# Chunk 0's scores over 128 rows with zero products between them, and raw weights that are loaded, measured and split at other steps

## The chip, the core and the metric

The kernel runs on one core of a Trainium2 chip. The metric is device time in microseconds. Three runs of the kernel before took 908.86, 908.33 and 905.04 us, so the median is 908.33 us. One further execution was profiled. It took 909.34 us, and its span from the first to the last instruction is 907.6 us.

The core has five engines that work beside each other: TensorE (PE, matrix products and transposes; its weight loads are the row PEld), VectorE (DVE), ScalarE (ACT), GpSimd (POOL) and SyncE (SP, which issues the transfers here). Each goes through its own list of instructions in a fixed order.

## The reference

Attention with a forget gate and causal mask, for 4 batches, 8 heads, 576 positions and head size 64, and behind it a mixture of 4 experts over the 2304 rows:

```
scores = scale * np.matmul(q, k.transpose(0, 1, 3, 2))
decay = cum[:, :, :, None] - cum[:, :, None, :]      # cum: running sum of log f
scores = np.where(causal, -1000000000.0, scores + decay)
attn = softmax(scores)                               # written out in the reference
x = (attn @ v), heads side by side                   # 2304 x 512
out += p[:, e:e+1] * (np.maximum(x @ w1[e], 0.0) @ w2[e])   # for e in 4 experts, w1 512x1024
```

All inputs and the output are float32.

## The kernel before

**Chunks and heads.** Rows are cut into nine chunks of 256. Chunks 0 to 3 are the first 256 positions of the four batches, chunks 4 to 8 the rest. The attention of a chunk is done by heads, two heads to a `Job`. Chunk 0 belongs to the first eight heads, h0 to h7 below (`FIRST` = 8).

**Startup.** `startup()` does chunk 0 in an order written out by hand. A head goes through: scores on PE (`qk_pe`, L631), their minimum on DVE (`qk_min`, L647), the exponential on ACT (`qk_exp`, L662), three transposes on PE (`tr_pe`, L768), a copy of these out of PSUM (`tr_copy`, L776 on ACT for even heads, L778 on DVE for odd ones), and the product with v (`av_pe`, L784). Two heads later a spread of the row sums follows (`spread`, L712). In turn s PE's list has the scores of head s+1, the transposes of head s and the v product of head s-1. For chunk 0 the decay is the 65th row of the operands: the tiles `first` hold 64 rows of q and k and one row of decays, and the scores are float32 products over these 65 rows. Ahead of all that `awake()` issues 18 products of zeros on PE.

**Experts, first sweep.** The weights of an expert come in four groups a half, a group in four units of 128x1024 (512 KB each). A `Step` is one half group on one chunk: first product (`l1`, L985 or L997), relu, second product (`l2`, L1040). The first `WIDE` = 4 groups (units 0 to 15) are used on chunk 0 as float32, straight from the loaded unit. For every later group a raw unit is loaded (`w_load`), the largest absolute value of it is taken on DVE (`w_top`, L310, or in halves through spare tiles), the four maxima give a scale (`w_scale`), and then `w_split` writes two float16 parts with ACT (L954) and DVE (L955). The steps count n = 0, 1, 2 ...; steps 0 to 7 are the wide ones, step 8 begins group 4.

**What sets the order.** Behind startup a scheduler places instructions, held back where the code says `issue_after`. `PACE` says which head's attention has begun by which step. Raw units live in two rings of four buffers, "wr" and "wk"; before, units 20 to 23 stand in two of the first, with two units in tiles of the accumulator. The list `loaded` with its step decides when a maximum is taken. `normalize()` (L458 to L461) turns the router's probabilities into shares on DVE; nothing before the end of the first step uses them. All transfers go through SP's one list, and each waits there for its buffer.

Of the kernel before, what the change touches and what calls it, by code (L numbers as in the profile page):

```python
# [19 lines left out]
CH = 256  # L20
# [63 lines left out]
def fused(ctx: ExitStack, tc: tile.TileContext, qk, v, f, probs, w, out):  # L84
# [57 lines left out]
    def awake():  # L142

        t = zero.bitcast(F16)
        ps = ps_a.tile([128, 512], F32, tag="a", name="awake")
        for _ in range(18):
            nc.tensor.matmul(out=ps, lhsT=t[:, :128], rhs=t, start=True, stop=True)

    def decays():
        nc.vector.memset(zero, 0.0)  # L150
        nc.sync.dma_start(out=fr, in_=f)
        first_tiles()
        first_raw(0)
# [13 lines left out]
        nc.gpsimd.memset(ones_r, 1.0)  # L167
        for n in range(1, NPR):
            nc.gpsimd.memset(jobs[n].whole[64:65, :, :CH], 8.0)
        for t in q2:  # L170
            nc.gpsimd.memset(t[64:66, :].bitcast(F32), 8.0)
        nc.vector.memset(ones, 1.0)
        nc.vector.tensor_scalar(
            out=fr, in0=fr, scalar1=1e-4, scalar2=1.0, op0=ALU.max, op1=ALU.min
        )
        for a, z in ((0, CH), (CH, S)):
            nc.scalar.activation(out=fr[:, a:z], in_=fr[:, a:z], func=AF.Ln)
            nc.vector.tensor_tensor_scan(
                out=ncum[:, a:z],
                data0=ones[:, a:z],  # L180
                data1=fr[:, a:z],
                initial=ncum[:, a - 1 : a] if a else 0.0,
                op0=ALU.mult,
                op1=ALU.subtract,
            )
            if a == 0:
                first_row(0)
# [130 lines left out]
    def w_peek(i):  # L318

        g, k = divmod(i, 4)  # L320
        t = xf_p.tile([128, 1024], F32, tag=f"xf{2 + i % 2}", name=f"wp{i}")
        nc.sync.dma_start(out=t, in_=w[i])
        at_step(step + 2, lambda: w_top(g, k, t))
        if k == 3:
            at_step(step + 2, lambda: scale(g))

    def w_half(i, k):

        g, n = divmod(i, 4)
        t = x_p.tile([128, 512], F32, tag="x", name=f"wp{i}_{k}")  # L330
        nc.sync.dma_start(out=t, in_=w[i, :, 512 * k : 512 * k + 512])

        def top():
            nc.vector.tensor_reduce(
                out=wmax[:, slot(g), k, n : n + 1],
                in_=t,
                op=ALU.max,
                axis=AX.X,
                apply_absolute_value=True,
            )  # L340

        at_step(step + 2, top)
        if (n, k) == (3, 1):
            at_step(step + 3, lambda: scale(g))

    def scale(g):
        a_, b_, c_ = w_scale(g)
# [117 lines left out]
    def first_tiles():  # L465

        slots = [
            x_.tile([128, 1024], F32, tag=t, name=f"first{n}")
            for n, (x_, t) in enumerate([(xf_p, f"xf{k}") for k in range(3)] + [(acc_p, "acc")] * 2)
        ]  # L470
        firsts["v"] = slots[3]
        vt = firsts[0] = slots[3].rearrange("p (r t h d) -> p r t h d", r=NPR, t=2, h=2)
        for j in jobs[:NPR]:
            r = slots[(4, 0, 1, 2)[j.pr]]
            j.whole = r.rearrange("p (h n) -> p h n", h=2)
            j.raw = {hh: j.whole[:, hh] for hh in range(2)}
            j.vr = vt[:, j.pr]
        nc.gpsimd.memset(jobs[0].whole[64:65, :, :CH], 8.0)

    def first_raw(n):  # L480
        j = jobs[n]
# [28 lines left out]
    class Job:  # L510
# [99 lines left out]
        def qk_pe(self, hh, its):  # L610

            at = 512
            for t in its:
# [3 lines left out]
                for n, (a, z) in enumerate(cuts):  # L617
# [282 lines left out]
        return st + qs + us  # L900


    wh, wl, wraw, loaded = {}, {}, {}, {}
    NS = 4 * len(GROUPS)

    def unit(n):
# [8 lines left out]

    def w_load(n):
        if n < 4 * WIDE and n not in wraw:
            if n % 4 < 2:
                wraw[n] = w_p.tile([128, 1024], F32, tag="w", name=f"w{n}")
            else:  # L920
                wraw[n] = wr_p.tile([128, 1024], F32, tag=("wr", "wk")[n % 2], name=f"wr{n}", bufs=4)
# [1 line left out]
                gate.append(nc.sync.dma_start(out=wraw[n], in_=w[unit(n)]))  # L923
        elif n in RAWS and n not in wraw:
            i = RAWS.index(n)
            if i in (6, 7):
                wraw[n] = acc_p.tile([128, 1024], F32, tag="acc", name=f"wr{n}")
            else:
# [4 lines left out]
            loaded[n] = step  # L933

    def w_pair(n):
        t = w_p.tile([128, 2, 1024], F16, tag="w", name=f"w{n}")
# [6 lines left out]
    def w_split(n):  # L943
# [22 lines left out]
        if i < len(RAWS):  # L966
            w_load(RAWS[i])

    acc = {}
# [500 lines left out]
    ]  # L1470
    starts = [next(n for n, t in enumerate(steps) if t.s == s) for s in range(len(GROUPS))]

    EARLY = (starts[-1] + 3, starts[-1] + 5)
    done_at = {}
    for n, (j, _) in enumerate(heads):
# [39 lines left out]
    def pace(n):  # L1515
# [8 lines left out]
            m += 1  # L1524
        upto(m)

    def startup():

        J = lambda h: heads[h] if 0 <= h < FIRST else (None, None)
# [6 lines left out]
            heads[0][0].qk_min(0, t)  # L1536
        for s in range(FIRST + 2):
            (m, mm), (j, hh), (i, ii), (k, kk) = J(s + 1), J(s), J(s - 1), J(s - 2)
            if s == 1:
                bound[2]()  # L1540
            if s == 2:
                bound[3]()
            if m:
# [2 lines left out]
                m.qk_pe(mm, m.its)  # L1546
                for t in m.its:
                    m.qk_min(mm, t)
            if j:
                for t in j.its:  # L1550
                    j.qk_exp(hh, t)
# [3 lines left out]
                j.tr_pe(hh)  # L1555
            if i:
                i.tr_copy(ii)
                i.av_pe(ii)
                if ii:
                    i.recip()  # L1560
# [1 line left out]
                k.fin()  # L1562
            if s == 0:
                bound[0]()
                bound[1]()
            for n in {0: (0, 1, 2), 1: (3,), 3: (4, 5)}.get(s, ()):
                w_load(n)
            if s == 0:
# [20 lines left out]
    for n in range(len(steps) + 1):  # L1589
# [4 lines left out]
        if 0 <= n - V_PEEK < NV:  # L1594
            v_peek(n - V_PEEK)
        with tc.issue_after(gate[-1].ins):
            if n < 4:
                w_peek(4 * WIDE + n)
            if n == 0:
                w_load(RAWS[6])  # L1600
                w_load(RAWS[7])
        for i, m in W_PEEK:
            if 0 <= n - m < 8:
                w_half(i + (n - m) // 2, (n - m) % 2)
        if cur is not None:
# [5 lines left out]
                weigh(cur.g, cur.c)  # L1611
            if n == 5:
                narrow_0()
            due = [m for m in loaded if WIDE < m // 4 < SWEEP_1 and loaded[m] < n][:2]
            off = starts[s] + (len(GROUPS[s][1]) > 1)
            turn = next((k for k in range(WIDE, SWEEP_1 - 1) if n == starts[k] - 1), None)
            if turn:
                due += [m for m in loaded if m // 4 == turn + 1 and m not in due]
            for m in due:
                del loaded[m]  # L1620
                behind(lambda: w_top(GROUPS[m // 4][0], m % 4, wraw[m]))
            chain = None
            if turn:
                chain = w_scale(turn + 1)
                behind(chain[0])
            for q in range(4):
                cur.l1(q)
# [26 lines left out]
        if cur is not None:  # L1654
            if chain:
                chain[2]()
            s = cur.s
            for k in range(2):
                if n == off + k and WIDE <= s + 1 < len(GROUPS):
                    with tc.issue_after(cur.last.ins):  # L1660
                        for i in range(2):
                            w_split(4 * s + 4 + 2 * k + i)
            if n < 7:
                for i in range(2):
                    w_load(2 * n + AHEAD_W + i)
            if n == starts[WIDE - 1]:
                w_load(RAWS[4])
                w_load(RAWS[5])
# [95 lines left out]
```

## Time and profile before

| | |
|---|---|
| three runs | 905.04, 908.33, 908.86 us, median 908.33 |
| profiled execution | 909.34 us, span 907.6 us |
| PE busy | 874.5 us, 96% of the span |
| DVE busy | 681.1 us, 75% |
| ACT, POOL busy | 511.2 us and 363.1 us |
| TensorE's granted clock, mean | 0.986 of full speed |

The page's second part cuts the span into 40 slices and gives the busy share of each engine and the granted clock in tenths. [...] The clock's column shows 1.0 until its first event, whatever it was before. The records of a matmul overlap with the next one's, so the time of one is read from start to start.

### The profile page before, as it was taken

Reading aid. Unit: us, or ns where it says so; the run is one execution under the profiler, and the core shown is the slowest. Engines: PE = TensorE matmul, PEld = TensorE weight load, DVE = VectorE, ACT = ScalarE, POOL = GpSimd, SP = SyncE. Lnnn points to the kernel's source line nnn. Section 1 sums busy time; section 2 is a strip of 40 time slices with the busy share of each in tenths; the row PEclk is TensorE's granted clock in tenths of the full one; section 3 lists DMA queues with packets and bytes.
Section 4 is the critical chain, followed back from the end, with each engine's and each line's share of the span. In section 5 each row is a group of like instructions: output and inputs, shape, how many; then the busy total and the mean of one; then the engine's idle time right before and its main releaser. Section 6 shows DMA issues by size and latency. Waiting matters only on the chain.

```text
span 907.6 us, 16252 instructions
## 1 busy us (share of the span) xinstructions
PE 874.5 (96%) x5681; PEld 562.2 (62%) x5681; DVE 681.1 (75%) x1483; ACT 511.2 (56%) x1063; POOL 363.1 (40%) x416
## 2 busy tenths in 40 slices
PE   6999979999999999999999999999989999999998
PEld 3666656666666766666676666644456654666547
DVE  4466779888888899877878985846788647886486
ACT  3354653566766885666668664456655445654350
POOL 2233421434232243232232220756788437884160
PEclk7699999999999999999999999999999999999999
DMA  7996796887999989896998964171223432240003
GB/s 225 405 223 178 218 278 166 242 277 204 285 236 223 230 285 317 200 216 151 256 281 230 288 117 101 47 256 69 94 71 116 139 117 70 70 139 25 24 0 94
DMA packets 166306, 162.50 MB, mean 179 GB/s; under 512 B 104824, under 2 KB 129456, under 8 KB 166224
## 3 DMA queue, kind: packets, MB, share of 16 engines
q1 hardware_dynamic: 166224, 161.46, 64.4%
q8 instruction: 45, 0.74, 0.3%
q14 instruction: 37, 0.30, 0.1%
HBM read 115.65 MB, written 21.64 MB: 151 GB/s over the span
## 4 chain that ended last, share of the span: by engine, by line
PE 25%; POOL 12%; DVE 8%; ACT 7%; issue 4%; DMA 2%; POOLq 0%; ACTq 0%; SPq 0%; DVEq 0%
PE y L1275 6%; PE m L1275 6%; PE l L997 5%; PE l L1040 5%; POOL s L1335 4%; POOL wt L1172 4%; POOL wu L1172 2%; PE s L631 1%; PE o L810 1%; ACT wt L1199 1%; DMA pt<-z 1%; DVE w L955 1%; DVE acc L1069 1%; DVE rl L1161 1%; ACT r L1321 1%
## 5 line engine op out<-in xcount | busy, mean ns | idle before, releaser
L997 PE MATMUL l<-y,w 128*128 128x256 f16 x1728 | 212.8, 273 | 2.5 <-DVE gl L1014 2.3
L997 PEld LDWEIGHTS <-w 128*128 128x128 f16 x1728 | 163.1, 98 | 44.7 <-issue 10.7
L1040 PE MATMUL l<-w,gh 128*128 128x512 f16 (+1 forms) x600 | 184.6, 392 | 1.1 <-DVE acc L1069 1.1
L576 POOL CAST q<-raw 64x320 fp32r<-64x320 f32 (+1 forms) x56 | 26.4, 472 | 227.2 <-issue 126.1
L662 ACT ACTIVATE p<-p,nm 128x576 f32<-128x576 f32 (+3 forms) x112 | 74.4, 665 | 73.9 <-DVE nm L647 63.8
L1040 PE MATMUL l<-w,gl 128*128 128x512 f16 x284 | 106.6, 379 | 1.3 <-DVE gl L1014 1.3
L1069 DVE SCALAR_TENSOR_TENSOR acc<-y,scg,acc 128x256 f32<-128x256 f32 (+1 forms) x164 | 81.2, 516 | 14.9 <-PE y L1275 14.7
L749 DVE SCALAR_TENSOR_TENSOR z<-p,rs,z 128x384 f16<-128x384 f32 (+3 forms) x128 | 80.1, 649 | 13.7 <-ACT z L748 11.3
L583 POOL TENSOR_TENSOR kl<-raw,hi 64x576 fp32r<-64x576 f32 (+1 forms) x56 | 65.2, 1164 | 60.1 <-ACT hi L574 56.1
L1275 PE MATMUL m<-rh,bs 128*128 128x512 f16 x256 | 86.4, 379 | 0.2 <-POOL bs L1204 0.2
L1040 PEld LDWEIGHTS <-gh 128*128 128x128 f16 x568 | 51.3, 98 | 49.2 <-issue 7.4
L647 DVE CUSTOM_DVE_ANT_0 p<-s,mask 128x384 f32<-128x384 f32 (+3 forms) x112 | 58.5, 531 | 25.0 <-PE s L631 24.4
L748 ACT ACTIVATE z<-p,rs 128x384 f16<-128x384 f32 (+3 forms) x128 | 69.7, 591 | 6.3 <-ACT p L662 2.3
L631 PE MATMUL s<-hi 128*128 128x288 f32 (+4 forms) x176 | 69.9, 409 | 1.8 <-DVE y L839 1.3
L1204 POOL TENSOR_TENSOR bs<-wt,bs 128x512 f16<-128x512 f32 x32 | 38.0, 1190 | 73.4 <-ACT bs L1203 73.0
L1275 PE MATMUL m<-rh,bw 128*128 128x512 f16 x191 | 64.5, 379 | 1.0 <-ACT r L1321 1.0
L1275 PEld LDWEIGHTS <-bs 128*128 128x128 f16 x384 | 37.5, 98 | 38.8 <-POOL bs L1204 0.7
L1009 ACT ACTIVATE gh<-l 128x512 f16<-128x512 f32 (+1 forms) x80 | 47.0, 587 | 24.3 <-PE l L997 18.3
L1014 DVE SCALAR_TENSOR_TENSOR gl<-l,gh 128x512 f16<-128x512 f32 x72 | 49.4, 686 | 14.7 <-ACT gh L1009 13.8
L1310 DVE SCALAR_TENSOR_TENSOR h<-s,h 128x512 f16<-128x512 f32 x40 | 46.3, 1164 | 17.8 <-ACT h L1309 17.5
L574 ACT ACTIVATE hi<-raw 128x896 fp32r<-128x896 f32 (+1 forms) x56 | 45.1, 810 | 23.7 <-issue 11.8
L1275 PEld LDWEIGHTS <-h 128*128 128x128 f16 x480 | 46.9, 98 | 14.8 <-issue 2.6
(386 smaller groups left out, 1750.9 us busy)
## 6 DMA issues: line engine op xcount, KB each, us to landing
wr<-in_w SPq DMA_DIRECT2D x66, 512.0 KB
wd<-w SPq DMA_DIRECT2D x32, 512.0 KB
w<-wd SPq DMA_DIRECT2D x32, 512.0 KB
raw<-in_qk SPq DMA_DIRECT2D x32, 448.0 KB
wp<-in_w SPq DMA_DIRECT2D x32, 256.0 KB
bv<-wd SPq DMA_DIRECT2D x32, 256.0 KB
bw<-wd SPq DMA_DIRECT2D x32, 256.0 KB
raw<-in_qk SPq DMA_DIRECT2D x24, 256.0 KB
```

Source lines behind the costliest of these rows:

```text
L583: nc.gpsimd.tensor_tensor(out=kl[:64, :wk], in0=r[:64, ko : ko + wk], in1=hi[:64, ko : ko + wk].bitcast(F32), op=ALU.subtract,)
L631: nc.tensor.matmul(out=ps[:, at : at + z - a], lhsT=lhsT, rhs=rhs, start=(m == 0), stop=(m == len(parts) - 1),)
L647: nc.vector.tensor_tensor_reduce(out=pt[:, a:z], in0=ps, in1=mask[:, m0 + a : m0 + z], scale=-0.125, scalar=BIG if n == 0 else nm[:, col : ...
L662: nc.scalar.activation(out=pt[:, :w_], in_=pt[:, :w_], func=AF.Exp, scale=-1.0, bias=self.nmax[hh][:, c : c + 1], accum_out=self.ssum[:, h ...
L748: nc.scalar.activation(out=o[:, 0], in_=x, func=AF.Copy, scale=sc)
L749: nc.vector.scalar_tensor_tensor(out=o[:, 1], in0=x, scalar=sc, in1=o[:, 0], op0=ALU.mult, op1=ALU.subtract)
L997: nc.tensor.matmul(out=self.l1p[:, fi, :], lhsT=lhsT, rhs=rhs[:, k, :], start=(k == 0 and m == 0), stop=(k == 3 and m == 2),)
L1014: self.last = nc.vector.scalar_tensor_tensor(out=self.gl, in0=self.l1p, scalar=0.0, in1=self.gh, op0=ALU.max, op1=ALU.subtract,)
L1040: matmul(out=l2[tt], lhsT=lhsT, rhs=rhs, start=(opens and fi == 0 and m == 0), stop=(closes and fi == 1 and m == len(parts) - 1),)
L1069: nc.vector.scalar_tensor_tensor(out=acc[c][:, tt, d0:d1], in0=ps, scalar=sc, in1=acc[c][:, tt, d0:d1], op0=ALU.mult, op1=ALU.add,)
L1172: nc.gpsimd.tensor_tensor(out=t[:, k - 1, :], in0=w_of(a), in1=w_of(z), op=op)
L1275: line.append(nc.tensor.matmul(**args))
```

## The change

- `awake()` issues 16 products of zeros and not 18.
- The tiles of chunk 0 are filled with zeros from row 64 on (four DVE memsets of 64x1024, `first_ends`), the 8.0 of row 64 is written behind that, and the scores of chunk 0 go over all 128 rows.
- `fill(ps, n)` issues n float16 products of 128x128 zeros (a corner of the mask that holds zeros) into columns 384 on of a head's transpose tile: four ahead of the transposes of each of the eight heads, four ahead of each v product; 64 in all.
- In startup the exponent chain of the first bound moves: its transposes (`bound[1]`) stand behind the scores of h2, its second product behind the v product of h0 (`bound[2]`).
- `normalize()` is held back until startup's last instruction.
- Raw units alternate over both rings. Units 16 and 17 are loaded at step 0, 18 and 19 at step 2, 20 and 21 at step 4, 22 and 23 at step 6 (`LOADS`). Splits of group 4 go to steps 3 and 4, of group 5 to steps 8 and 9 (`SPLITS`). Maxima stand at steps of a table (`TOPS`, `SCALES`), of four units through spare tiles. Units 14 and 15 stand in accumulator tiles. Since `w_load` looks for a unit in `wraw`, and a split takes it out, the loop `w_load(2 * n + AHEAD_W + i)` loads units 16 to 19 once more at steps 5 and 6.
- `PACE` asks for one head more by steps 8 and 18.

```diff
-PACE = ((8, 19), (18, 27), (28, 35))
+PACE = ((8, 20), (18, 28), (28, 35))
...
-        for _ in range(18):
+        for _ in range(16):
...
+    def fill(ps, n):
+
+        t = mask.bitcast(F16)
+        for _ in range(n):
+            nc.tensor.matmul(
+                out=ps[:, 384:], lhsT=t[:, :128], rhs=t[:, :128], start=True, stop=True
+            )
...
+    def first_ends(n):
+        nc.vector.memset(jobs[n].whole[64:], 0.0)
+        nc.gpsimd.memset(jobs[n].whole[64:65, :, :CH], 8.0)
...
-                        r = self.raw[hh][:65]
+                        r = self.raw[hh]
...
             ps = self.tp[hh] = ps_2.tile([128, 512], F32, tag="l2", name=f"t{self.nm}_{hh}")
+            fill(ps, FILL[0])
...
                 i.tr_copy(ii)
+                fill(i.tp[ii], FILL[1])
                 i.av_pe(ii)
...
-    normalize()
+    with tc.issue_after(fins[1].ins):
+        normalize()
...
-                wraw[n] = wr_p.tile(
-                    [128, 1024], F32, tag=("wr", "wk")[i % RAW >= 4], name=f"wr{n}", bufs=4
-                )
+            wraw[n] = wr_p.tile([128, 1024], F32, tag=("wr", "wk")[i % 2], name=f"wr{n}", bufs=4)
...
+    LOADS = {2: (18, 19), 4: (20, 21), 6: (22, 23)}
+    TOPS = {7: (20, 21), 8: (24, 25), 9: (26, 27), 12: (28, 29), 14: (30, 31)}
+    SCALES = {3: 4, 7: 5, 10: 6, 15: 7}
+    SPLITS = {3: (16, 17), 4: (18, 19), 8: (20, 21), 9: (22, 23)}
```

The first place is PE's list in startup, in the turns of h2 to h4 before (`s` scores, `t` transposes, `o` the v product, `b` the spread; the numbers are pair and head).

```order
L631 MATMUL s_2_0_0_0_0_344<-first_185 128x128
L631 MATMUL s_2_0_0_0_0_344<-first_185 128x256
L712 MATMUL b_0_0_351<-ident,x_first_175 128x128 x2
L768 MATMUL t_1_0_1_354<-ident,p_1_0_1_0_309 128x128
L768 MATMUL t_1_0_1_354<-ident,p_1_0_1_1_310 128x128 x2
L784 MATMUL o_1_0_359<-pth_first,first_187 64x256
L784 MATMUL o_1_0_359<-pth_first,first_187 64x128
```

The same stretch of PE's list in the changed kernel, of which the eight rows of the first fill end in the transposes:

```order
L153 LDWEIGHTS mask
L153 MATMUL t_1_0_1_376<-mask 128x128
L782 MATMUL t_1_0_1_376<-ident,p_1_0_1_0_323 128x128
L782 MATMUL t_1_0_1_376<-ident,p_1_0_1_1_324 128x128 x2
L153 LDWEIGHTS mask
L153 MATMUL t_1_0_0_333<-mask 128x128
L153 LDWEIGHTS mask
L153 MATMUL t_1_0_0_333<-mask 128x128
L153 LDWEIGHTS mask
L153 MATMUL t_1_0_0_333<-mask 128x128
L153 LDWEIGHTS mask
L153 MATMUL t_1_0_0_333<-mask 128x128
```

Four loads and products of zeros stand ahead of the transposes and four ahead of the v product that follows; the order of the real products is as it was.

The second place is DVE's list around the scores of h3 before (`psum_` and `prob` are `normalize`, `pth_first` is the copy of h1's transposes).

```order
L288 TENSOR_SCALAR vsc<-ux_240 128x1
L458 TENSOR_REDUCE psum__116<-pr_t 128x18
L459 TENSOR_SCALAR psum__116<-psum__116 128x18
L460 RECIPROCAL psum__116<-psum__116 128x18
L461 TENSOR_TENSOR prob<-pr_t,psum__116 128x72
L647 ISA p_1_0_1_0_309,nm_1_0_1_311<-s_1_0_1_0_0_312,mask 128x128
```

And in the changed kernel:

```order
L296 TENSOR_SCALAR vsc<-ux_242 128x1
L660 ISA p_1_0_1_0_323,nm_1_0_1_325<-s_1_0_1_0_0_326,mask 128x128
L660 ISA nm_1_0_1_325 128x1
L660 ISA p_1_0_1_1_324,nm_1_0_1_325<-s_1_0_1_0_0_326,mask 128x256
L660 ISA nm_1_0_1_325 128x1
L792 COPY pth_first<-t_0_0_1_295 128x384
```

The four instructions of `normalize` have left this place; they stand behind the last multiplication of startup now.

The third place is SP's list in the changed kernel at steps 5 and 6 (`wr` a raw unit, `pt` a transfer that transposes attention weights, `kl` and `raw` the inputs of a later head). `wr_1073`, `wr_1075` and `wr_1163` here, and `wr_1165` some rows on, are the second loads of units 16 to 19; nothing reads them.

```order
L545 DMA raw_1_0_0_1063<-in_qk 128x512
L943 DMA wr_1073<-in_w 128x1024
L943 DMA wr_1075<-in_w 128x1024
L545 DMA raw_1_0_1_1101<-in_qk 128x512
L774 DMA_TRANSPOSE pt_3_0_0_952<-z_613 128x2x128
L774 DMA_TRANSPOSE pt_3_0_0_952<-z_613 128x4x128
L943 DMA wr_1163<-in_w 128x1024
L774 DMA_TRANSPOSE pt_3_0_1_1041<-z_614 128x2x128
L774 DMA_TRANSPOSE pt_3_0_1_1041<-z_614 128x4x128
```

Before, the rows around the same transfers hold no raw unit:

```order
L532 DMA raw_1_0_0_963<-in_qk 128x512
L546 DMA kl_1_0_0_961<-ncd 2x256
L761 DMA_TRANSPOSE pt_3_0_0_870<-z_549 128x2x128
L761 DMA_TRANSPOSE pt_3_0_0_870<-z_549 128x4x128
L761 DMA_TRANSPOSE pt_3_0_1_941<-z_550 128x2x128
L761 DMA_TRANSPOSE pt_3_0_1_941<-z_550 128x4x128
```

Raw units now stand between the transposing transfers of the last head of chunk 1.

## Rows read from the trace of the kernel before

**Rows 1.** The page's first part: busy us, share of the span and instructions

```profile
PE 874.5 (96%) x5681; PEld 562.2 (62%) x5681; DVE 681.1 (75%) x1483; ACT 511.2 (56%) x1063; POOL 363.1 (40%) x416
```

**Rows 2.** Busy time by stretches: from:to, length, engines, clock, DMA share, GB/s

```profile
12.50:36.50 24.00, 20.18 (x64) 13.32 (x64) 6.69 (x36) 6.46 (x24) 1.10 (x3) 0.50 0.90 344
41.80:95.00 53.20, 53.20 (x241) 36.17 (x240) 36.06 (x115) 26.60 (x76) 19.39 (x34) 1.00 0.76 201
95.00:145.00 50.00, 43.31 (x274) 28.58 (x273) 39.29 (x94) 26.16 (x65) 13.12 (x20) 1.00 0.85 257
...
9.00:12.50 3.50, 1.15 (x6) 0.58 (x6) 3.12 (x12) 2.60 (x10) 0.00 (x0) 1.00 0.83 236
22.00:29.60 7.60, 7.60 (x24) 5.01 (x24) 1.60 (x9) 1.89 (x9) 0.40 (x1) 0.50 1.04 406
```

**Rows 3.** PE's timeline in startup: start, us, engine, line, operation, tiles, xcount, idle before

```profile
1.17 6.31 PE L147 MATMUL awake<-zero 128*128 128x512 f16 x18 [1.17 <-DVE zero L150]
7.40 1.55 PE L631 MATMUL s<-first 65*128 65x128 f32 x8
...
21.88 1.54 PE L784 MATMUL o<-pth_first,first 128*64 128x256 f32 x4 [3.26 <-DVE pth_first L778]
...
25.22 0.85 PE L768 MATMUL t<-ident,p 128*128 128x128 f32 x3
26.00 1.54 PE L784 MATMUL o<-pth_first,first 128*64 128x256 f32 x4
27.47 1.65 PE L631 MATMUL s<-first 65*128 65x128 f32 x4
28.91 0.85 PE L768 MATMUL t<-ident,p 128*128 128x128 f32 x3
...
39.39 0.49 PE L768 MATMUL t<-ident,p 128*128 128x128 f32 x3
39.81 1.66 PE L784 MATMUL o<-pth_first,first 128*64 128x256 f32 x8
...
41.79 3.62 PE L985 MATMUL l<-x,w 128*128 128x256 f32 x16
```

**Rows 4.** PE's waits from 8 to 45 us: who for whom, us, times, longest

```profile
PE o L784 <- DVE pth_first L778: 3.3, 1, 3.3
PE o L784 <- DVE ptl_first L778: 1.4, 2, 0.9
PE topx L242 <- DVE ux L235: 1.3, 1, 1.3
```

**Rows 5.** DVE's timeline in startup

```profile
1.17 0.54 DVE L172 MEMSET ones<- 32x576 f32 x1
8.45 0.29 DVE L647 CUSTOM_DVE_ANT_0 p<-s,mask 128x128 f32<-128x128 f32 x1 [3.10 <-PE s L631]
19.80 0.23 DVE L458 TENSOR_REDUCE psum__116<-pr_t 128x18 f32<-128x72 f32 x1 [4.37 <-DMA pr_t<-in_probs]
```

**Rows 6.** The page's groups: float16 weight loads of 128x128

```profile
L1040 PEld LDWEIGHTS <-gh 128*128 128x128 f16 x568 | 51.3, 98 | 49.2 <-issue 7.4
```

**Rows 7.** PE's waits from 95 to 145 us

```profile
PE l L997 <- DVE gl L1014: 2.3, 1, 2.3
PE s L631 <- DVE y L839: 1.3, 1, 1.3
PE l L1040 <- DVE acc L1069: 0.8, 1, 0.8
PE l L1040 <- DVE gl L1014: 0.4, 1, 0.4
```

**Rows 8.** DVE's waits from 95 to 145 us

```profile
DVE wmax L310 <- DMA wr<-in_w: 6.0, 4, 3.5
```

**Rows 9.** Clock, DMA share and GB/s while the first weights are loaded

```profile
22.00:50.00 28.00, 0.74 1.03 398
```

**Rows 10.** SP's waits from 60 to 140 us, for raw units

```profile
SPq L932 <- PE o L810: 0.4, 1, 0.4
```

More of the change, by code (lines that the diff above doesn't have):

```diff
@@ L167, in decays @@
         nc.gpsimd.memset(ones_r, 1.0)
-        for n in range(1, NPR):
-            nc.gpsimd.memset(jobs[n].whole[64:65, :, :CH], 8.0)
         for t in q2:
@@ L186, in decays @@
             if a == 0:
+                for n in range(1, NPR):
+                    first_ends(n)
                 first_row(0)
@@ L342, in w_half, with w_maxed @@
         at_step(step + 2, top)
-        if (n, k) == (3, 1):
+        if (n, k) == (3, 1) and g < WIDE:
             at_step(step + 3, lambda: scale(g))
+    def w_maxed(n):
+        behind(lambda: w_top(GROUPS[n // 4][0], n % 4, wraw[n]))
     def scale(g):
@@ L477, in first_tiles @@
             j.vr = vt[:, j.pr]
-        nc.gpsimd.memset(jobs[0].whole[64:65, :, :CH], 8.0)
+        first_ends(0)
+    def first_ends(n):
+        nc.vector.memset(jobs[n].whole[64:], 0.0)
+        nc.gpsimd.memset(jobs[n].whole[64:65, :, :CH], 8.0)
     def first_raw(n):
@@ L900, in head_steps @@
         return st + qs + us
-    wh, wl, wraw, loaded = {}, {}, {}, {}
+    wh, wl, wraw = {}, {}, {}
     NS = 4 * len(GROUPS)
@@ L917, in w_load @@
         if n < 4 * WIDE and n not in wraw:
-            if n % 4 < 2:
+            if n >= 4 * WIDE - 2:
+                wraw[n] = acc_p.tile([128, 1024], F32, tag="acc", name=f"wa{n}")
+            elif n % 4 < 2:
                 wraw[n] = w_p.tile([128, 1024], F32, tag="w", name=f"w{n}")
@@ L925, in w_load @@
             i = RAWS.index(n)
-            if i in (6, 7):
-                wraw[n] = acc_p.tile([128, 1024], F32, tag="acc", name=f"wr{n}")
-            else:
-                wraw[n] = wr_p.tile(
-                    [128, 1024], F32, tag=("wr", "wk")[i % RAW >= 4], name=f"wr{n}", bufs=4
-                )
+            wraw[n] = wr_p.tile([128, 1024], F32, tag=("wr", "wk")[i % 2], name=f"wr{n}", bufs=4)
             nc.sync.dma_start(out=wraw[n], in_=w[unit(n)])
-            loaded[n] = step
     def w_pair(n):
@@ L965, in w_split @@
         i = RAWS.index(n) + RAW
-        if i < len(RAWS):
+        if n // 4 < SWEEP_1 - 2:
+            at_step(step + 1, lambda: w_load(RAWS[i]))
+        elif i < len(RAWS):
             w_load(RAWS[i])
@@ L1471, in fused @@
     starts = [next(n for n, t in enumerate(steps) if t.s == s) for s in range(len(GROUPS))]
+    LOADS = {2: (18, 19), 4: (20, 21), 6: (22, 23)}
+    TOPS = {7: (20, 21), 8: (24, 25), 9: (26, 27), 12: (28, 29), 14: (30, 31)}
+    SCALES = {3: 4, 7: 5, 10: 6, 15: 7}
+    SPLITS = {3: (16, 17), 4: (18, 19), 8: (20, 21), 9: (22, 23)}
+    for s_ in range(5, len(GROUPS) - 1):
+        for k_ in range(2):
+            n_ = starts[s_] + (len(GROUPS[s_][1]) > 1) + k_
+            SPLITS.setdefault(n_, []).extend(4 * s_ + 4 + 2 * k_ + i_ for i_ in range(2))
     EARLY = (starts[-1] + 3, starts[-1] + 5)
@@ L1525, in pace @@
         upto(m)
+    FILL = (4, 4)
     def startup():
@@ L1548, in startup @@
                     m.qk_min(mm, t)
+            if s == 1:
+                bound[1]()
             if j:
@@ L1564, in startup @@
                 bound[0]()
-                bound[1]()
+            if s == 1:
+                bound[2]()
             for n in {0: (0, 1, 2), 1: (3,), 3: (4, 5)}.get(s, ()):
@@ L1596, in fused @@
         with tc.issue_after(gate[-1].ins):
-            if n < 4:
-                w_peek(4 * WIDE + n)
             if n == 0:
-                w_load(RAWS[6])
-                w_load(RAWS[7])
+                for i in range(2):
+                    w_load(RAWS[i])
+                for i in range(2):
+                    w_peek(RAWS[2 + i])
+            for i in {2: (6,), 3: (7,)}.get(n, ()):
+                for k in range(2):
+                    w_half(RAWS[i], k)
+        if n == 2:
+            for i in range(2):
+                w_maxed(RAWS[i])
         for i, m in W_PEEK:
@@ L1613, in fused @@
                 narrow_0()
[L1614 to L1621, printed above, removed]
             chain = None
-            if turn:
-                chain = w_scale(turn + 1)
+            for m in TOPS.get(n, ()):
+                w_maxed(m)
+            if n in SCALES:
+                chain = w_scale(SCALES[n])
                 behind(chain[0])
@@ L1657, in fused @@
             s = cur.s
[L1658 to L1662, printed above, removed]
+            for k, m in enumerate(SPLITS.get(n, ())):
+                with tc.issue_after(cur.last.ins):
+                    w_split(m)
             if n < 7:
@@ L1665, in fused @@
                     w_load(2 * n + AHEAD_W + i)
-            if n == starts[WIDE - 1]:
-                w_load(RAWS[4])
-                w_load(RAWS[5])
+            for m in LOADS.get(n, ()):
+                w_load(m)
             for p, m in enumerate(EARLY):
```

4 lines of the change are left out of this document (removed).

## The prediction, made before the changed kernel had run

> **What bounds the kernel now.** I read the page first. PE is busy 96% of the span [rows 1], so a microsecond counts where PE is idle or slow. Then the busy time by stretches. [...] From 41.8 to 95 us it is never idle [rows 2]. [...]
>
> In startup PE's timeline shows what the half clock costs, since each kind of work occurs at both levels [rows 3]. At half clock the scores of a head take 1.44 us from their start to the next start (27.47 to 28.91), its transposes 0.78 (25.22 to 26.00), its v product 1.47 (26.00 to 27.47). At the upper level they take 0.78 (1.55 for two heads from 7.40), 0.42 (39.39 to 39.81) and 0.83 (1.66 for two). What PE did before the clock changed: it fell at 12.6 us behind a stretch in which PE was busy 1.15 of 3.5 us. It stayed at half from 22.0 to 29.6 us though PE's records fill that whole stretch with 65-row scores, transposes and 64-column v products [rows 2]. It rose at 36.5 us.
>
> [...]
>
> PE's waits name the rest of startup: 3.3 us for the DVE copy of h1's transposes, 1.3 for the exponent chain, 1.4 for two other copies [rows 4]. DVE's own timeline says why the first is there: the first instruction of `normalize` sat 4.37 us for the probabilities' transfer, and the minimum of h3 and that copy stood behind it [rows 5].
>
> **The change part by part.** I work from the profiled execution's 909.3 us, which is 1.0 above the median of the three runs.
>
> *Clock.* In the half-clock stretch lie 5.4 scores, 5 sets of transposes, 5 v products. At the upper level they save 5.4 x 0.66 + 5 x 0.36 + 5 x 0.64 = 8.6 us [rows 3]. Scores over 128 rows cost no more than over 65: the 65-row products take 1.55 us for 768 columns (2.0 ns a column), the 128-row ones of the first expert step 3.62 us for 8 x 256 columns (1.8 ns) [rows 3].
>
> The trace shows that transposes and float32 v products at half clock filled 22.0 to 29.6 us together with scores, and no rise [rows 2]. [...] The clock held behind 36.5 us with transposes among the work, and this trace does not settle it further. [...]
>
> *Waits.* The 3.3 us go, as `normalize` leaves that place; the probabilities are there by 20 us, and it now runs beside the first expert products. What is late next on PE is the copy of an odd head, which stands on DVE behind the minimum of the head two further on. Of the 1.3 us of the exponent chain I count 0.9 as gone: its last product now has the v product of h0 in front.
>
> *New waits.* At the upper clock PE gets to a v product sooner than DVE finishes that copy. The longest such wait at full clock was 0.9 us [rows 4]. Four odd heads at 0.6 make 2.4, of which 1.4 are there already: 1.0 more (from 0 to 2.2).
>
> *Fills.* Sixteen groups of four products of 128 columns. The trace has none of that shape. By columns alone a group is 512 columns, 0.21 us. If each weight load of 98 ns [rows 6] is not hidden, 0.60. Four groups stand in the waits just named and cost nothing; 12 x 0.30 = 3.6 us. The ends are 12 x 0.21 = 2.5 and 16 x 0.60 = 9.6. I take a value near the lower end, since loads of this kind lie beside products in their row. [...]
>
> *Memsets.* A DVE memset of 576 columns took 0.54 us [rows 5], so 1024 columns make 0.96. The first lies beside the wait for f. The other three make 2.9 us between the two scans, and DVE sat idle for 3.10 us just behind these [rows 5]. So nothing; without that cover up to 2.9. The two zero products less cost nothing either, as the next scores' minimum waits for DVE.
>
> Startup: 8.6 + 3.3 + 0.9 - 1.0 - 3.6 = 8.2 us sooner at the first expert product, at 33.6 and not at 41.8. The ends are 8.6 + 4.2 - 2.2 - 9.6 = 1 and 8.6 + 4.2 - 2.5 = 10.3.
>
> *Maxima and splits.* From 95 to 145 us four PE waits end in DVE work: 2.3, 1.3, 0.8 and 0.4, in all 4.8 [rows 7]. In the same stretch DVE itself sat 6.0 us in four maxima of raw units which had not landed [rows 8], with gates, sums and splits queued behind. The change loads these units at steps 2 to 6, and moves eight split halves of group 4 and 5 into the time before, where DVE is busy 36.06 of 53.2 us and the DMA share is 0.76 [rows 2]. I take three quarters of the 4.8: 3.6 (from 0 to 4.8).
>
> *Second loads.* Units 16 to 19 come twice: 2 MB that nobody reads, which at 398 GB/s [rows 9] is 5.2 us of transfers. They fall where the share is 0.76, so they are hidden but for what they hold up in SP's list. The longest wait of a raw unit for its buffer was 0.4 us [rows 10]; four of these are 1.6, of which I count 1.0 (from 0 to 5.2).
>
> *Pace.* One head more by steps 8 and 18 moves attention work, and takes none away: nothing, with the early stretch's free ACT and DVE time as cover.
>
> Sum: 909.3 - 8.2 - 3.6 + 1.0 = 898.5 in the profile's terms, 897.5 against the median. By the ends: 909.3 - 1 - 0 + 5.2 = 913.5 and 909.3 - 10.3 - 4.8 = 894.2; less the 1.0 these are 912.5 and 893.2. That PE's other waits get shorter too can add some microseconds below.
>
> **The rivals.**
>
> *A, the forecast.* The clock holds or dips only shortly, and the lead stays to the end. For it: PE is busy 96%, so a lead in its list is lost only where something else limits. About 897.5, on its own from 890 to 902.
>
> *B, the lead is given back to transfers.* From 22 to 50 us the DMA share is 1.03 at 398 GB/s [rows 9], so the transfers can't end sooner by much, and PE would meet units and heads' inputs that have not landed. Against it: the first units are issued ahead of that stretch, and a wide step needs 1 MB, 2.6 us of transfers, while its first products alone take 3.62 us [rows 3]. If it takes 5 of the 8.2 us: 902.5.
>
> *C, the change doesn't do what it says.* Transposes and waits of odd heads let the clock fall as at 12.6 us and it stays at half. Then 8.6 us stay lost, fills cost 16 x 0.43 = 6.9 less the 1.4 us of gaps; 909.3 - 4.2 + 5.5 - 3.6 + 1.0 = 908.0, or 907 against the median. Against it: the fills make PE busier just where it was idle.
>
> *D, slower.* SP's list is one queue. The second loads of units 16 to 19 stand in it ahead of transposing transfers of chunk 1's last head and wait for buffers that a later product frees; v products wait, PE idles for some microseconds at about 80 to 100 us, and the clock falls behind such a pause as it did at 12.6. A half-clock stretch as long as startup's costs 8.6 again: 909.3 - 8.2 + 5.2 + 8.6 = 914.9, 914 against the median. It decides from the point where a pause is as long as that of 9.0 to 12.5 us. Against it: SP's waits for raw units were short [rows 10].
>
> **How the numbers follow.** A 0.67, B 0.17, C 0.09, D 0.07. I name A's 897. A difference below about 0.5% (4.5 us) can't be told from none here. Faster by more than that means below 903.8: nearly all of A, two thirds of B, a quarter of C, in all 0.81. Within it: the rest of B, half of C and a little of D, 0.11. Slower: 0.08. The range that leaves out 2 in 10 goes from 888, for waits that shorten beyond those counted, to 906, which takes in B and leaves C and D out.
>
> **What would show it.** Right: a granted clock of 1.00 from 12.5 us on; a group of four fills of 0.2 to 0.4 us; no wait of DVE for the probabilities; the first L985 product (its line in the changed kernel) at 32 to 35 us; waits of PE between 85 and 135 us below 3 us; DVE maxima that wait for no raw unit. Wrong: half clock again in startup (C), idle PE between 34 and 60 us on weights or inputs (B), SP waiting for a raw unit ahead of a transposing transfer with PE waiting behind (D). If the lead at 34 us is there and missing at 900, the loss lies between and its stretch names it.

## The result and the profile after

The changed kernel takes 892.93 us, the median of four runs (891.13 to 893.98), against 907.58 for four runs of the kernel before on the same chip. The ratio is 0.984, with a 95% interval of 0.981 to 0.987. The profiled execution took 893.55 us with a span of 891.8; before it was 909.34 with 907.6. So 15.8 us are gone between the two traces.

The stretches that [rows 2] gave, in the changed kernel (columns as there), and one more for the dip of the clock:

```profile
9.00:12.50 3.50, 2.89 (x25) 1.90 (x22) 3.48 (x15) 3.27 (x13) 0.00 (x0) 1.00 0.80 229
12.50:36.50 24.00, 22.03 (x154) 16.90 (x153) 12.99 (x48) 9.73 (x33) 5.17 (x10) 1.00 0.97 357
41.80:95.00 53.20, 53.20 (x246) 36.01 (x245) 36.48 (x114) 28.87 (x76) 17.44 (x28) 1.00 0.90 281
95.00:145.00 50.00, 47.23 (x322) 30.92 (x320) 40.90 (x116) 23.98 (x65) 15.32 (x21) 0.97 0.96 247
103.30:106.70 3.40, 3.40 (x24) 2.43 (x23) 3.40 (x8) 0.78 (x2) 0.59 (x1) 0.56 0.86 287
```

Startup runs at a granted clock of 1.00 throughout (0.50 from 12.5 to 36.5 us before), PE is busy 2.89 of the 3.5 us ahead of 12.5 (1.15 before), and the turn from the wide groups to the split ones, at 95 to 145 us, has 2.8 us of idle PE where it had 6.7. The DMA share between 41.8 and 95 us rose from 0.76 to 0.90. What is new is a short half clock at 103 us, granted 0.50 from 102.90 to 106.32.

PE's timeline in startup (columns as in [rows 3]; L153 are the zeros, L997 the first expert product):

```profile
7.40 1.55 PE L644 MATMUL s<-first 128*128 128x128 f32 x8 [1.26 <-DMA first<-ncum]
...
15.56 0.38 PE L153 MATMUL t<-mask 128*128 128x128 f16 x4 [0.65 <-DVE pth_first L792]
15.87 0.86 PE L798 MATMUL o<-pth_first,first 128*64 128x256 f32 x4
16.67 0.92 PE L644 MATMUL s<-first 128*128 128x128 f32 x4
17.43 0.38 PE L725 MATMUL b<-ident,x_first 128*128 128x128 f32 x2
17.64 0.39 PE L153 MATMUL t<-mask 128*128 128x128 f16 x4
17.87 0.50 PE L782 MATMUL t<-ident,p 128*128 128x128 f32 x3
18.20 0.39 PE L153 MATMUL t<-mask 128*128 128x128 f16 x4
18.52 0.86 PE L798 MATMUL o<-pth_first,first 128*64 128x256 f32 x4
...
31.77 2.54 PE L997 MATMUL l<-x,w 128*128 128x256 f32 x11
```

The first expert product starts at 31.77 and not at 41.79. From one start to the next a group of zeros takes 0.23 (17.64 to 17.87) or 0.32 us (18.20 to 18.52). The 3.26 us wait is gone; in its place an odd head waits 0.65 for its copy, and the zeros behind that copy wait with it, since they write the same PSUM tile.

DVE's waits between 95 and 145 us, all that there are:

```profile
DVE s L660 <- ACT s L675: 6.1, 2, 5.9
DVE z L762 <- ACT z L761: 2.2, 1, 2.2
DVE s L660 <- PE s L644: 0.4, 1, 0.4
```

No maximum waits for a raw unit there any more (6.0 us in [rows 8]). PE's waits in that stretch:

```profile
PE o L824 <- DMA pt<-z: 2.0, 2, 1.3
PE topw L250 <- DVE uw L243: 0.7, 1, 0.7
```

The first of these has a tail. PE's timeline around it:

```profile
100.99 0.30 PE L824 MATMUL o<-pt,v 128*64 128x256 f16 x1 [0.66 <-DMA pt<-z]
101.22 0.27 PE L229 MATMUL topw<-ident,wtop 128*2 128x128 f32 x1
101.33 0.49 PE L1009 MATMUL l<-y,w 128*128 128x256 f16 x3
103.16 1.17 PE L824 MATMUL o<-pt,v 128*64 128x256 f16 x11 [1.34 <-DMA pt<-z]
104.26 2.36 PE L1009 MATMUL l<-y,w 128*128 128x256 f16 x11
```

Eleven expert products take 2.36 us here at half clock, and ten took 1.25 at 99 us at 1.00. The half clock set in 0.26 us before the end of the second wait. SP's longest line of waits between 85 and 104 us is at loads of raw units:

```profile
SPq L943 <- DMA wr<-in_w: 1.7, 2, 1.0
```

Of these only 0.7 us stand ahead of the transfers that PE waits for: the second load of unit 18 waits there until that of unit 16 has landed. The 1.0 us are those of unit 22 behind the transfers, which waits for the second load of unit 18. SP's list where the 0.7 us end:

```profile
96.67 0.33 SPq L943 DMA_DIRECT2D wr<-in_w  x1
97.09 3.01 SPq L774 DMA_TRANSPOSE pt<-z  x2
```

Where the lead arises, from the starts of the same products in both traces: 10.0 us at the first expert product, 12.1 at the last wide one's first product, 13.1 from 245 to 340 us, 13.4 at the split product of 406 us, 15.3 from 531 us to the end.

### The profile page after: what moved, and what is told of

It reads as the page before. It is cut to its first block, busy times and chain, and to the rows that moved or that the text cites. A ratio compares the mean times of both kernels' runs of the same rounds, so it can differ in the third digit from the quotient of the medians.

```text
span 891.8 us, 16401 instructions
## 1 busy us (share of the span) xinstructions
PE 868.8 (97%) x5743; PEld 560.6 (63%) x5743; DVE 683.1 (77%) x1489; ACT 509.7 (57%) x1063; POOL 367.6 (41%) x416
## 4 chain that ended last, share of the span: by engine, by line
PE 29%; POOL 12%; DVE 6%; ACT 6%; issue 3%; DMA 1%; SPq 0%; POOLq 0%; DVEq 0%; ACTq 0%
PE y L1287 7%; PE l L1052 6%; PE l L1009 6%; PE m L1287 6%; POOL s L1347 5%; POOL wt L1184 4%; PE s L644 2%; POOL wu L1184 2%; PE o L824 2%; ACT wt L1211 1%; DVE acc L1081 1%; DVE rl L1173 1%; ACT r L1333 1%; ACT bs L1215 1%; POOL bs L1216 1%
## 5 line engine op out<-in xcount | busy, mean ns | idle before, releaser
L1009 PE MATMUL l<-y,w 128*128 128x256 f16 x1728 | 215.8, 274 | 0.0
L1322 DVE SCALAR_TENSOR_TENSOR h<-s,h 128x512 f16<-128x512 f32 x40 | 46.3, 1164 | 17.8 <-ACT h L1321 17.5
L1026 DVE SCALAR_TENSOR_TENSOR gl<-l,gh 128x512 f16<-128x512 f32 x72 | 49.3, 684 | 13.8 <-ACT gh L1021 12.8
```

The lines of the kernel that those rows point to most:

```text
L1009: nc.tensor.matmul(out=self.l1p[:, fi, :], lhsT=lhsT, rhs=rhs[:, k, :], start=(k == 0 and m == 0), stop=(k == 3 and m == 2),)
L1026: self.last = nc.vector.scalar_tensor_tensor(out=self.gl, in0=self.l1p, scalar=0.0, in1=self.gh, op0=ALU.max, op1=ALU.subtract,)
```

## The experiments

Each kernel is the one before or the changed one with the edit that is named. The kernel before ran beside each batch, at 907.9 to 908.2 us.

**Which part holds the clock.** Six kernels take the startup part apart.

*No zeros in the gaps.*

```
-    FILL = (4, 4)
+    FILL = (0, 0)
```

> The changed kernel without the sixteen groups of four zero products; the 128-row scores stay. Theory 1 (the gaps need the zeros): the granted clock falls to 0.50 in startup as it did before, some 12 to 24 us of it, and the first expert product comes 5 to 9 us later than the changed kernel's 31.8 us, at 37 to 41; time 897 to 902. Theory 2 (128-row scores and the absence of the long waits hold the clock by themselves): clock 1.00, first expert product at 30.5 to 32 us, time 891 to 893, the same as the change within what can be told.

893.66 us, ratio 0.983 (0.979 to 0.987). Its startup, by stretches:

```profile
9.00:12.50 3.50, 2.75 (x15) 1.63 (x15) 3.48 (x15) 3.28 (x13) 0.00 (x0) 1.00 0.78 231
12.50:36.50 24.00, 20.98 (x115) 15.73 (x114) 13.67 (x49) 9.74 (x33) 5.19 (x10) 1.00 0.96 353
```

The clock holds without zeros, and the first expert product comes at 29.27: 2.5 us earlier, outside the span given for either theory. Sixteen groups cost 2.5 us, 0.16 each. The end does not show it. In the profiled execution the lead over the changed kernel is still 2.4 us at 384, and goes here:

```profile
386.18 2.70 PE L824 MATMUL o<-pt,v 128*64 128x320 f16 x27 [2.01 <-DMA pt<-z]
388.81 2.09 PE L1009 MATMUL l<-y,w 128*128 128x256 f16 x12
```

There 2.01 us are spent in one wait for a transposing transfer, with 3.4 us of half clock behind, in this one execution. The three unprofiled runs, with a mean clock of 1.00, took 890.08 to 894.43; what they lost is not seen.

*Zeros, but 65 rows.*

```
-                        r = self.raw[hh]
+                        r = self.raw[hh][:65]
```

> The changed kernel with chunk 0's scores over 65 rows as before; zeros in the gaps stay. Theory 1 (zeros in the gaps hold the clock): clock 1.00 in startup, first expert product at 31.8, time 892 to 894. Theory 2 (the 128 rows hold it): clock 0.50 for some 12 to 24 us, first expert product at 37 to 41 us, time 897 to 902.

892.11 us, ratio 0.983 (0.979 to 0.987), clock 1.00 from start to end, first expert product at 31.77. The zeros hold it as well.

*Neither* (both edits).

> The changed kernel with 65-row scores and without the zeros in the gaps; normalize stays held back, and the weights part stays. Either theory of the clock (rows or zeros): clock 0.50 in startup as before, of 24 us or less, first expert product at 37 to 41 us, time 897 to 902. The rival: before's half clock came from the 3.5 us stretch with little work and from the 3.3 us wait, and with the wait gone the clock holds or comes back early: below 12 us of half clock, first expert product at 31 to 35 us, time 891 to 896.

904.77 us, ratio 0.996 (0.993 to 0.999), ten runs between 900.6 and 910.9:

```profile
9.00:12.50 3.50, 2.90 (x15) 1.63 (x15) 3.48 (x15) 3.27 (x13) 0.00 (x0) 1.00 0.81 226
12.50:36.50 24.00, 21.30 (x86) 14.43 (x85) 9.65 (x45) 9.14 (x32) 3.02 (x7) 0.72 0.97 354
```

Half clock from 16.2 to 29.8 us, first expert product at 35.02. So one of the two is needed and either is enough, and 65-row scores with PE as busy ahead of 12.5 do not hold it. The end is 12 us behind the changed kernel though the first expert product is only 3.2 behind: this trace has three more half-clock stretches, at 108, 211 and 504 us, 13.7 us in all.

*128 rows alone.* The kernel before, with

```
-                        r = self.raw[hh][:65]
+                        r = self.raw[hh]
...
+        nc.vector.memset(jobs[n].whole[64:], 0.0)
```

> The kernel before with chunk 0's scores over 128 rows and the memsets that they need, and nothing else: no zeros in the gaps, normalize where it was, so the 3.3 us wait for the copy and the stretch with PE busy 1.15 of 3.5 us are still there. Theory 1 (128 rows hold the clock even over these waits): clock 1.00 in startup, first expert product about 8.6 us sooner, at 33 to 34; time 898 to 901. Theory 2 (the waits bring the clock down whatever the products): half clock for 14 us or more, first expert product at 37 to 42; time 902 to 908.

903.83 us, ratio 0.996 (0.994 to 0.998), first expert product at 38.0, half clock for 10.2 us in two pieces from 13.9 on. Neither theory in full.

```profile
9.00:12.50 3.50, 1.42 (x6) 0.43 (x5) 3.40 (x14) 2.80 (x10) 0.00 (x0) 1.00 0.79 225
12.50:36.50 24.00, 18.36 (x80) 12.46 (x80) 8.71 (x46) 8.19 (x30) 1.44 (x4) 0.79 0.93 346
```

PE is again idle for most of 9.0 to 12.5 us, as in [rows 2], and the clock falls behind that in spite of the 128 rows. The second piece, from 20.7 us on, begins in the other long pause of startup, the wait that `normalize` causes:

```profile
21.47 1.54 PE L797 MATMUL o<-pth_first,first 128*64 128x256 f32 x4 [3.55 <-DVE pth_first L791]
```

*Zeros alone*, in the kernel before:

```
+            fill(ps, FILL[0])
...
+                fill(i.tp[ii], FILL[1])
```

> The kernel before with the sixteen groups of four zero products and nothing else: scores over 65 rows, normalize where it was, the 3.3 us wait still there but for what a group of zeros covers of it. By what 128 rows alone showed (half clock for 10.2 of the 20 us from 13.9 on, first expert product at 38.0, 903.8): half clock for 7 to 14 us, first expert product at 37 to 40, 902 to 906. Rival (zeros are better than rows, as a group lies in each long wait): clock 1.00 throughout, first expert product at 34 to 36, 900 to 902.

907.32 us, ratio 0.999 (0.996 to 1.001): startup as expected, the time with no gain that can be measured. Half clock from 10.6 to 17.5 and from 20.9 to 27.7, first expert product at 39.95. Both falls come in or behind the same two pauses.

```profile
9.00:12.50 3.50, 1.45 (x8) 0.60 (x6) 3.10 (x12) 2.57 (x10) 0.00 (x0) 0.73 0.84 247
```

*Only `normalize` held back*, in the kernel before:

```
-    normalize()
+    with tc.issue_after(fins[1].ins):
+        normalize()
```

> The kernel before with one edit: normalize is held back to the end of chunk 0's last head. Theory 1 (the wait of 3.3 us goes and the clock stays at half as before, the wait being its price and not its cause): first expert product at 38 to 39, time 904 to 905. Theory 2 (this edit alone brings the 65-row clock to what the kernel with neither rows nor zeros showed, a half-clock stretch of 13.7 us from 16.2 on): first expert product at 35.0, time 901 to 902 and with the same scatter. Rival (the lead is lost on the way): 907 to 909.

908.48 us, ratio 0.999 (0.997 to 1.002). First expert product at 38.90, 2.9 us sooner, as Theory 1 had it, with 20.5 us of half clock; the time is that of its rival. In the trace the gain is gone by 106 us: PE waits 2.1 us for the weights' maxima at 101 us, and a dip of the clock follows at 101.3. It is back at 2.0 us by 200 us there, but that execution is the fastest of the ten (905.57). PE's waits from 85 to 145 us begin with

```profile
PE l L997 <- DVE gl L1014: 2.3, 1, 2.3
PE topw L242 <- DVE uw L235: 2.1, 1, 2.1
```

Startup taken together (half clock before 37 us, first expert product; the order is that of `x_bound`'s parts with `normalize` held back):

| kernel | half clock, us | first product at, us | time, us |
|---|---|---|---|
| before | 23.9 | 41.8 | 907.6 |
| held `normalize` alone | 20.5 | 38.9 | 908.5 |
| 128 rows alone | 10.2 | 38.0 | 903.8 |
| zeros alone | 13.7 | 40.0 | 907.3 |
| order, 65 rows, no zeros | 13.7 | 35.0 | 904.8 |
| order and 128 rows | 0 | 29.3 | 893.7 |
| order and zeros | 0 | 31.8 | 892.1 |
| all (the change) | 0 | 31.8 | 892.9 |

The times compare only within the upper four and within the lower four rows, since the lower four have the weights part of the change too. That part does not act on startup: with the startup part alone the first expert product stands at 31.77 us, with the weights part alone at 41.42 (below). The lower four also have two products of zeros less at the very start, which was not tried apart. Which half of the order counts, `x_bound`'s or `normalize`, was not tried with rows or zeros; but with 128 rows alone the first fall follows the pause that `x_bound`'s order fills, and the second begins in the wait that `normalize` causes, so both may be needed.

**The two halves of the change.** *Startup part alone*: the changed kernel's startup with before's weights part.

> The kernel before with the whole startup part of the change (128-row scores, zeros in the gaps, normalize held back, the order of x_bound's parts), and the weights part as before. Theory 1 (the lead of 10.0 us at the first expert product is kept where nothing else limits, and the weights part adds its own 3 to 5): first expert product at 31.8, time 897 to 899. Rival (the weights part is what lets the lead through: with before's order of loads the units have not landed, and PE or DVE waits take the lead back by 145 us): 901 to 905.

900.27 us, ratio 0.992 (0.989 to 0.995), first expert product at 31.77. PE's waits from 85 to 145 us begin with

```profile
PE l L1053 <- ACT gh L1022: 3.5, 1, 3.5
```

The lead goes from 10.0 to 7.7 us by 305 us, with 6.8 us of half clock from 116 us on in between, and is 8.9 at 531. Neither theory's time: it lies between them, and what is lost is lost in the turn.

*Weights part alone* (rings, loads, splits, maxima, pace; before's startup):

> The changed kernel with the startup part of before: the weights part (rings, loads, splits, maxima, pace) alone. Theory 1 (parts add up): first expert product at 41.8 as before, half clock of about 24 us in startup, then 3 to 5 us gained by 145 us and the end at 902 to 905. Rival (the second loads and the pause they cause cost what the maxima give): 906 to 909, no change. A second rival (the later 2 us at 487 to 531 us belong to the weights part too): 900 to 902.

902.62 us, ratio 0.994 (0.992 to 0.996), first expert product at 41.42. PE's busy time from 95 to 145 us is

```profile
95.00:145.00 50.00, 47.62 (x316) 30.99 (x315) 37.69 (x99) 23.90 (x64) 12.33 (x21) 1.00 0.98 254
```

so 4.3 us of idle PE less than in [rows 2], and the time is within what Theory 1 gave. By the ratios the parts alone give 7.2 and 5.6 us of 908, in all 12.8, and together 14.5; the intervals are too wide to tell the two from each other.

**The second loads.** *Without them:*

```
-                    w_load(2 * n + AHEAD_W + i)
+                    if 2 * n + AHEAD_W + i < 4 * WIDE:
+                        w_load(2 * n + AHEAD_W + i)
```

> The changed kernel without the second loads of units 16 to 19, which nobody reads. Theory 1 (they stand ahead of the transposing transfer for which PE waited 2.0 us at 99 to 103 us, and the dip of the clock to 0.56 behind it follows from that): both waits go, clock 1.00 at 95 to 110 us, 3 to 4 us faster than the change, 889 to 890. Theory 2 (the transposing transfer is late anyway, since its heads come later relative to PE): the wait and the dip stay, time 892 to 893.

893.39 us, ratio 0.984 (0.979 to 0.988): no change. The clock has no dip there (1.00), the waits for `pt` shrink to 0.9, and another wait is longer than they are:

```profile
PE l L1052 <- DVE gl L1026: 1.7, 1, 1.7
PE o L824 <- DMA pt<-z: 0.9, 2, 0.7
```

The second of the two waits for `pt` is the one that shrinks, from 1.34 to 0.15 us:

```profile
101.85 0.68 PE L824 MATMUL o<-pt,v 128*64 128x256 f16 x11 [0.15 <-DMA pt<-z]
```

So that wait goes with the second loads, as Theory 1 had it, and its price does not hold: in the trace 2.0 us are ahead at 104 us, and the wait for the gates takes most of that at 120. How the loads make the transfer late is not settled. In the second trace of the change (below) PE waits 1.3 us there too, though the load held SP only 0.2 us; the transfer stood 2.2 us for DVE:

```profile
SPq L774 <- DVE nm L660: 3.2, 2, 2.2
```

Nor is it shown that the dip followed from the loads, since by its mean clock the change runs without it in some executions.

*Without them and without zeros* (both edits above):

> The changed kernel without the zeros in the gaps and without the second loads of units 16 to 19. If the 2.5 us of the zeros and the pause behind the second loads are both real in the end's time, 888 to 890 and thus faster than the change; if the stages behind give leads beyond the change's back (the transposing transfer at 386 us took the zeros' 2.5 us, another wait took the second loads'), 891 to 894, the same as the change.

889.20 us, ratio 0.979 (0.976 to 0.982), six runs from 888.23 to 892.32. This beats the change. The turn, and all that PE waits for from 85 to 145 us:

```profile
95.00:145.00 50.00, 50.00 (x354) 32.72 (x353) 44.93 (x118) 27.06 (x67) 17.44 (x25) 1.00 0.71 183
```

```profile
PE o L824 <- DMA pt<-z: 0.5, 1, 0.5
```

Each edit alone moved the time by nothing that can be measured, both together by some 3.8 us. In the traces the lead over the change is 2.5 us at the first expert product, 4.6 at 104 us and 5.4 at the end. Why neither the gates nor the transposing transfer of 386 us takes it here is not shown.

*The changed kernel again*, against that version:

> The changed kernel once more, to compare it with the version without the zeros in the gaps and without the second loads (889.2). If that version is really faster, this run gives 892 to 894 again and the 3 to 4 us between them stay. Rival: the change's four runs were on the high side by chance, and it comes out at 889 to 891, the same as that version. Its granted clock tells whether the dip at 103 us belongs to every execution: with a mean of 0.998 it dips once, with 1.000 not at all.

893.02 us, ratio 0.984 (0.981 to 0.987), six runs from 891.94 to 894.26. The profiled one and one more had a mean clock of 0.998, one 0.999, three 1.000, so the dip at 103 us does not come in every execution. The two at 0.998 took 893.4 and 894.3, the others 891.9 to 894.1. The kernel before ran at 907.86 beside this one and at 908.15 beside that version. So the difference of 3.8 us is there, and the dip is at most a part of it.

**The price of the zeros.** *Eight instead of four in each group:*

```
-    FILL = (4, 4)
+    FILL = (8, 8)
```

> The changed kernel with eight zero products in each of the sixteen groups, so the price of a group doubles and nothing else changes. Theory 1 (a group costs 0.2 to 0.3 us where PE is not idle anyway, and idle gaps of the odd heads take up 1.9 us): first expert product 1.5 to 3.5 us later than 31.8, at 33.3 to 35.3, clock 1.00; time 893 to 896. Rival (leads of startup beyond some size are given back on the way, so a delay of startup is partly taken up by waits that go): the first product as above, and the time 892 to 894, not to be told from the change.

894.33 us, ratio 0.985 (0.981 to 0.989), clock 1.00 in startup, first expert product at 34.31. Four more cost 2.5 us again. PE's waits in startup are 3.6 us without zeros, 2.5 with four, 1.6 with eight (copies of odd heads, exponentials and, without zeros, 0.3 of the exponent chain; summed from each trace's waits). So the raw price of four products is (2.5 + 1.1)/16 = 0.23 and then (2.5 + 0.9)/16 = 0.21 us, and a quarter to a third lies in waits. The time lies in Theory 1's range and just outside its rival's, too near the change's to decide. The traces speak for the rival: the delay of 2.5 us is there until 95 us and gone at 110, and this execution has neither the waits for `pt` nor the dip of the clock there.

## Why the prediction was right or wrong

The forecast of 897.0 us lies 4.1 above the result, and A's mechanism is the one that ran. In the profile's terms the sum said 898.5, and 893.55 came out. The 5.0 us between are 1.8 in startup, about 0.8 in the turn and 2.4 late.

Startup is best read in the kernel without zeros, from the first scores to the first expert product. The first row is before, the second that kernel (columns as in [rows 2]):

```profile
7.40:41.79 34.39, 27.24 (x101) 17.79 (x100) 12.99 (x61) 11.30 (x42) 2.24 (x7) 0.65 0.90 336
7.52:29.27 21.75, 17.99 (x99) 12.11 (x100) 13.37 (x59) 11.28 (x41) 2.44 (x7) 1.00 0.88 307
```

**Clock: right.** No half clock in startup. A head's scores take 0.76 us, start to start (16.67 to 17.43), against 1.44. PE's busy time falls by 9.2 us, where 8.6 were counted. The prediction's reason was too simple, though: it took the rows and zeros to do it, and traced the fall to the idle stretch ahead of 12.5 us without making anything of it. The table shows that both matter. Rows or zeros without the order bring the half clock to 10.2 or 13.7 us; the order without them to 13.7; the order with either to 0. That the order was part of the change is luck as far as the forecast goes: it counted `normalize` for 3.3 us of waiting and the exponent chain for 0.9, and neither for the clock.

Rival C had the transposes among its causes. In the kernel with 128 rows and no zeros startup holds 1.00 with transposes between its float32 products, with PE busy 20.98 of 24 us. So in this mix they did not bring it down; no run here has transposes by themselves. Zeros by themselves stand at the start of the trace before: the first eleven products of `awake` take 0.42 us each (1.17 to 5.80 us, start to start), the others 0.22 (5.80 to 7.10), so PE came to its faster pace there with nothing but zeros.

**Waits: right.** Without zeros PE's idle time in startup falls by 3.4 us, and 3.3 + 0.9 - 1.0 = 3.2 were counted. The 3.3 us went. Of the exponent chain's 1.3 us 0.9 went, as counted. Odd heads wait 2.6 us in three places (4 heads at 0.6 were expected), so new waits cost 1.2. And a wait at the head of that chain went which the prediction did not list:

```profile
PE topx L221 <- DVE xsc L294: 0.6, 1, 0.6
```

**Fills: too dear.** 3.6 us were counted, 2.5 were paid. A group's raw price is 0.21 to 0.23 us, where 0.30 was counted, and the 1.1 us by which waits shrink are the cover. That cover was described wrongly: the group behind a copy waits for that copy, and it is the group ahead of the transposes that shortens the wait. From start to start some groups take 0.32 us, but the transposes behind a group then take 0.33 (17.87 to 18.20) and not 0.42 as in [rows 3]. The raw price measured is 53 to 57 ns a product with its load. The 0.21 us that the prediction gave 512 columns is close to the 0.22 of the later `awake` products, and the 0.43 in rival C to the 0.42 of the first ones; the 0.60 for loads that are not hidden is seen in no run.

**Memsets: right.** The first scores start at 7.40 in both traces.

Clock, waits and fills together make 0.6 + 0.2 + 1.1 = 1.9, and startup beat its forecast by 1.8 us (the first scores of the kernel without zeros start 0.1 later).

**Maxima, splits and second loads: right in kind.** PE idles 2.8 us in the turn, not 6.7, and no maximum waits for a raw unit there. The weights part alone takes 4.3 us of idle time from this stretch (3.6 counted). The 4.8 us of [rows 7] were not all of PE's waits there that end in DVE work; the longest that was left out:

```profile
PE topw L242 <- DVE uw L235: 1.1, 1, 1.1
```

The second loads did what rival D described, in small: one held SP 0.7 us ahead of transposing transfers (0.2 in the second trace), PE waited 2.0 for those, of which 1.1 went without the loads, and the clock fell in that execution, for 3.4 us and not for 24. But taking them out returned nothing while the zeros stood, and 4.5 us (893.66 to 889.20) without zeros. So the 1.0 counted for them is not a term that stands by itself.

**The late 2.4 us were not foreseen.** Most of them appears at 487 to 531 us, where PE's idle time falls from 2.6 to 0.9 us between 500 and 560. Before, all of it is two waits for transposing transfers. The weights part alone gains 1.4 there in its trace and the startup part alone 0.4; but `normalize` held back alone gains 1.2 there too, with nothing changed so late. These are single executions, and half-clock dips at 504 us came and went in other traces; which edit earns it, if any does, stays open.

**B and C** are ruled out by the lead, which is 10.0 us at the first expert product and 12.5 to 15.5 from 245 us to the end, and by the clock. B's mechanism is real elsewhere: in its profiled execution the 2.5 us that the version without zeros gains in startup are given back at 386 us to a transposing transfer.

## What to carry to other kernels

The half clock of this startup, in which each step of a head waits for the one before it on another engine, had two conditions in these runs: pauses, and products that did not hold the level behind them. Mending one alone (rows, zeros or the whole order) left 10.2 to 13.7 us of half clock, and mending both left none, so such edits are worth trying together and not only one by one. Padding products with zero rows, from 65 to 128, or filling gaps with zero products, did the same job here; padding cost PE no time (at 1.00 a head's scores take 0.76 us with 65 rows and with 128), zeros cost 2.5 us, so the padding goes first and the zeros come out again if it suffices. Where several waits end close together, an edit that takes one away can show nothing until the next is taken too: two edits worth nothing alone were worth 3.8 us together.

## What the runs showed that was not expected

- Waits of PE of 1.3 to 2.1 us, for transposing transfers at 103 us (the change) and 386 us (no zeros) and for the weights' maxima at 101 us (`normalize` alone), each came with 3.4 us of half clock, which set in about the end of the wait, in a phase otherwise at 1.00. The length of the wait alone did not decide: behind 2.3 us before (the first of [rows 7]) and behind 1.7 in the kernel without second loads the clock stayed at 1.00. And by its mean clock the same program dips in some executions and not in others.
- The kernel that enters the expert phase 3.2 us late ends 12 us late. The spread of its runs is 10 us, and 3 us in the changed kernel: the dips, and not the startup alone, make the time uncertain. Of its runs, the two at the lowest mean clock (0.981) are the two slowest, at 908.7 and 910.9.
- From 41.8 to 95 us the DMA share rose from 0.76 to 0.90 without a microsecond of idle PE. Two megabytes that nobody read were not measurable in the time until the zeros were gone too.
